# Decode step with attention and SwiGLU: layernorm steps on ScalarE, weight loads requeued, gate products moved, normalised input padded to 64 columns

## The chip, the cores and the metric

The kernel runs on one core of a Trainium2 chip. A core has TensorE (PE, matrix products; its weight loads are shown apart as PEld), VectorE (DVE), ScalarE (ACT), GpSimd (POOL) and SyncE (SP, which here issues DMAs and waits). Products land in PSUM, everything else lives in SBUF, and inputs come from HBM through 16 DMA engines. The metric is the device time of one execution in microseconds, as the median of several runs. One further execution is profiled; its span runs from the first instruction to the last.

## The reference

Four batch rows of one token each. The token is layer-normalised, and the result feeds an attention step over the last 4096 cached positions and a SwiGLU feed-forward; both are added to the input.

```python
B, D, F = 4, 512, 1792
Hq, Hkv, Sk, Dh = 32, 8, 16384, 128        # W = 4096, 4 query heads per K/V head
xn = (x - mean(x)) / sqrt(var(x) + 1e-5)
q  = (xn @ wq)                              # [B, Hq, Dh]
k, v = k_cache[:, :, Sk-W:, :], v_cache[:, :, Sk-W:, :]
o  = softmax(q k^T * Dh**-0.5) v
out = x + (o @ wo) + (silu(xn @ w_gate) * (xn @ w_up)) @ w_down
```

All inputs are bf16. K and V of the window are 33.5 MB each, W_q and W_o 4.2 MB each, and W_gate, W_up and W_down 1.8 MB each: some 81 MB, each byte read once.

## The kernel before

The order of work on every engine is written out by hand, and the engines meet through semaphores.

**Start.** ScalarE's queue loads x. VectorE sums x (L253), forms D*x - sum as `xc` (L255), ScalarE squares `xc` and accumulates (L239), VectorE forms the variance (L257), ScalarE takes the root (L241), VectorE the reciprocal (L259) and the scaled `xn` (L261). TensorE transposes `xn` in four pieces into PSUM (L336), VectorE copies them as `XnT` (L263), and TensorE multiplies 128 blocks of W_q with `XnT`, four columns each, into `q_ps` (L344). VectorE spreads q into `QZ` (L267), a table of 64-column blocks that are zero outside the 8 columns in use. Meanwhile GpSimd builds constants: masks, identity matrices, a zeroed `QZ` (L197); it raises `s_const` to 1 (L199), fills `P` with ones (L200), zeroes 12288 columns of `VB` (L201) and raises `s_const` to 2.

**The loop.** There are 32 pairs of batch row and K/V head, taken two at a time: `ND` = 16 steps, each with one 2 MB load of K and one of V. `KB` and `VB` hold two steps each. In one step TensorE transposes the first half of K (32 blocks, L357) while VectorE copies the results to `KT` (L276); takes the row maxima of the step before (L373); makes the second half of the products with V for two steps back, called PV here (L391, 64 moving columns each); makes the scores of the first half (L367); adds the shift by the maximum (L377), after which ScalarE takes the exponential (L244); and repeats transposes, PV and scores for the other halves. The first PV works on the ones and zeros that GpSimd left, and its end is the first count of `s_pv`. VectorE sums and inverts the denominators and scales the output into `OT` (`norm`, L290).

**The queue.** Nearly all loads go through SP's queue in one written order (L217 to L230): W_q, K of steps 0 and 1, W_down, V of step 0, then K and V in turn, the last V, W_gate, W_up and W_o in four pieces. Before each K from step 2 on, SP waits until both halves of the K two steps back are transposed (`s_tr`); before each V until the PV that frees its buffer has ended (`s_pv`). Everything further down the queue waits behind that.

**The end.** After the loop TensorE does the last maxima, the second half of PV for step 14, the shift for step 15, then all of PV for step 15 (L427, L428), the gate products (`up_gate`, L429: 56 blocks, four columns each, a weight block read with a stride of 14 elements), waits for the last normalisation (L430), transposes `OT` (L432) and regroups it (L438), makes the up products (L441), adds x, then multiplies W_down (L448) and W_o (L454), the latter as its four pieces land. VectorE copies the result out (L326), and two DMAs store it.

Of the kernel before, what the change touches and what calls it, by code (L numbers as in the profile page):

```python
# [3 lines left out]
BF16 = mybir.dt.bfloat16  # L4
FP32 = mybir.dt.float32
ALU = mybir.AluOpType
# [4 lines left out]
def bass_parallel_sum__sliding_block_cached__swiglu_ffn__decode_kernel(  # L11
# [18 lines left out]
    NC = D // 128  # L30
# [42 lines left out]
    xc = sb("xc", [B, D], FP32)  # L73
    xsq = sb("xsq", [B, D], FP32)
    xn = sb("xn", [B, D], FP32)
    st_sum = sb("st_sum", [B, 1], FP32)
    st_var = sb("st_var", [B, 1], FP32)
    st_std = sb("st_std", [B, 1], FP32)
    st_rstd = sb("st_rstd", [B, 1], FP32)
    XnT = sb("xnT", [128, NC, B], BF16)  # L80
    den = sb("den", [128, C], FP32)
    OT = sb("oT", [128, B, REP + HQ], BF16)
    OB = sb("oB", [32, B, Dh], BF16)
# [16 lines left out]
    O_wide = ps_O[:, 0:WIDE]  # L100
    den_ps = ps_O[:, 128:256]
    q_ps = ps_acc[:, 0:HQ * B]
    xT_ps = ps_acc[:, 128:128 + NC * B]
    mt_ps = ps_acc[0:C, 0:128]
    gate_ps = ps_kt[0][:, 0:NF * B]
    up_ps = ps_kt[1][:, 0:NF * B]
# [3 lines left out]
    def sem(name):  # L110
        return nc.alloc_semaphore(name=name)
# [12 lines left out]
    s_ss = sem("s_ss")  # L124
    s_var = sem("s_var")
    s_std = sem("s_std")
    s_xn = sem("s_xn")
    s_xT = sem("s_xT")
    s_xnT = sem("s_xnT")
# [36 lines left out]
    with nc.Block() as block:  # L166

        @block.gpsimd
        def _(eng):
            eng.memset(ident[:], 0.0)  # L170
            eng.memset(I4[:], 0.0)
            eng.memset(I8[:], 0.0)
            eng.memset(I4w[:], 0.0)
            eng.memset(rep[:], 0.0)
            eng.memset(ones[:], 1.0)
            eng.memset(mkr[:], -BIG)
            eng.memset(mkc[:], 1.0)
            eng.drain()
            eng.affine_select(I4[:], I4[:], pattern=[[-1, B]], compare_op=ALU.not_equal,
                              fill=1.0, base=0, channel_multiplier=1)  # L180
            eng.affine_select(ident[:], ident[:], pattern=[[-1, 128]], compare_op=ALU.not_equal,
                              fill=1.0, base=0, channel_multiplier=1)
            eng.affine_select(I8[:], I8[:], pattern=[[-1, C]], compare_op=ALU.not_equal,
                              fill=1.0, base=0, channel_multiplier=1)
            eng.affine_select(I4w[:], I4w[:], pattern=[[-1, 64]], compare_op=ALU.not_equal,
                              fill=1.0, base=0, channel_multiplier=1)

            eng.affine_select(rep[:], rep[:], pattern=[[1, REP], [-1, 128]], compare_op=ALU.not_equal,
                              fill=1.0, base=0, channel_multiplier=REP)

            eng.affine_select(mkr[:], mkr[:].rearrange("j (q b) -> j q b", b=2),
                              pattern=[[0, 64], [-1, 2]], compare_op=ALU.not_equal,
                              fill=0.0, base=0, channel_multiplier=1)
            eng.affine_select(mkc[:], mkc[:].rearrange("j (b h) -> j b h", b=2),
                              pattern=[[-1, 2], [0, REP]], compare_op=ALU.is_equal,
                              fill=0.0, base=0, channel_multiplier=1)
            eng.memset(QZ[:], 0.0)  # L197
            eng.drain()
            eng.engine_nop().then_inc(s_const, 1)  # L199
            eng.memset(P[:], 1.0)  # L200
            eng.memset(VB[:, HKN:], 0.0)  # L201
            eng.drain()
            eng.engine_nop().then_inc(s_const, 1)  # L203
            eng.engine_nop().then_inc(d_v[1], 16)

        @block.sync
        def _(eng):
            def load_k(d):
                if d >= 2:
                    eng.wait_ge(s_tr, 2 * NG * (d - 1))  # L210
                eng.dma_start(KB[:, d % 2 * KVN:(d % 2 + 1) * KVN], kv_ap(A_k_cache, d)).then_inc(d_k[d % 2], 16)

            def load_v(d):
                eng.wait_ge(s_pv, d + 1)
                eng.dma_start(VB[:, d % 2 * KVN:(d % 2 + 1) * KVN], kv_ap(A_v_cache, d)).then_inc(d_v[d % 2], 16)

            eng.dma_start(WQ[:], wq_ap).then_inc(d_wq, 16)  # L217
            load_k(0)
            load_k(1)
            eng.dma_start(WD[:], wd_ap).then_inc(d_wd, 16)  # L220
            load_v(0)
            for d in range(2, ND):
                load_k(d)
                load_v(d - 1)
            load_v(ND - 1)
            eng.dma_start(WG[:], wg_ap).then_inc(d_wg, 16)
            eng.dma_start(WU[:], wu_ap).then_inc(d_wu, 16)
            for n in range(len(d_wo)):
                a, b = WO_CUTS[n], WO_CUTS[n + 1]
                eng.dma_start(WO[:, a:b, :], wo_ap[:, a:b, :]).then_inc(d_wo[n], 16)  # L230
            eng.wait_ge(s_y, 1)
            eng.dma_start(out_ap[0], y[0:B, :]).then_inc(d_out, 16)
            eng.wait_ge(d_out, 32)

        @block.scalar
        def _(eng):
            eng.dma_start(X[:], x_ap).then_inc(d_x, 16)
            eng.wait_ge(s_xc, 1)
            eng.activation(xsq[:], xc[:], ACT.Square, accum_out=st_sum[:, 0:1]).then_inc(s_ss, 1)  # L239
            eng.wait_ge(s_var, 1)  # L240
            eng.activation(st_std[:], st_var[:], ACT.Sqrt).then_inc(s_std, 1)  # L241
            for d in range(-1, ND):
                eng.wait_ge(s_sh, d + 2)
                eng.activation(P[:, d % 2 * PS:d % 2 * PS + SN], ps_S[d % 2][:], ACT.Exp, scale=SCALE).then_inc(s_p, 1)  # L244
            eng.wait_ge(s_gate, 1)
            eng.activation(ex[:], gate_ps.rearrange("p (t b) -> p t b", b=B), ACT.Exp, scale=-1.0).then_inc(s_ex, 1)
            eng.wait_ge(s_y, 1)
            eng.dma_start(out_ap[1], y[64:64 + B, :]).then_inc(d_out, 16)

        @block.vector  # L250
        def _(eng):
            eng.wait_ge(d_x, 16)
            eng.tensor_reduce(st_sum[:], X[:], AX.X, ALU.add)  # L253
            eng.drain()
            eng.tensor_scalar(xc[:], X[:], float(D), st_sum[:, 0:1], ALU.mult, ALU.subtract).then_inc(s_xc, 1)  # L255
            eng.wait_ge(s_ss, 1)
            eng.tensor_scalar(st_var[:], st_sum[:], 1.0 / D, EPS * D * D, ALU.mult, ALU.add).then_inc(s_var, 1)  # L257
            eng.wait_ge(s_std, 1)
            eng.reciprocal(st_rstd[:], st_std[:])  # L259
            eng.drain()  # L260
            eng.tensor_scalar(xn[:], xc[:], st_rstd[:, 0:1], None, ALU.mult).then_inc(s_xn, 1)  # L261
            eng.wait_ge(s_xT, 1)
            eng.tensor_copy(XnT[:], xT_ps.rearrange("p (c b) -> p c b", b=B)).then_inc(s_xnT, 1)  # L263
            eng.wait_ge(s_const, 1)
            eng.wait_ge(s_q, 1)
            for bp in range(2):
                last = eng.tensor_copy(  # L267
# [61 lines left out]
        def _(eng):  # L329
            def mm(o, l, r, start=False, stop=True):  # L330
                return eng.matmul(o, l, r, start=start, stop=stop, skip_group_check=True)  # L331
# [9 lines left out]
            for c in range(NC):  # L341
                for h in range(HQ):
                    a = (c * HQ + h) * Dh
                    last = mm(q_ps[:, h * B:(h + 1) * B], WQ[:, a:a + Dh], XnT[:, c, :],  # L344
                              start=(c == 0 and h == 0))
            last.then_inc(s_q, 1)

# [32 lines left out]
            def pv(bank, s, n):  # L380
                p = bank * PS
                if s == 0:
                    eng.wait_ge(d_v[bank], n[0])
                    eng.wait_ge(s_p, n[1])
                    eng.wait_ge(s_nrm, n[1])
                    for j in range(SN // 128):
                        mm(den_ps, ones[:], P[:, p + 128 * j:p + 128 * (j + 1)], start=(j == 0))
                for t in range(HT):
                    a = bank * KVN + s * HKN + 128 * t
                    o = p + C * (s * HT + t)  # L390
                    last = mm(O_wide, VB[:, a:a + 128], P[:, o:o + WIDE], start=(s == 0 and t == 0))  # L391
                if s == 1:
                    last.then_inc(s_pv, 1)
# [24 lines left out]
            def up_gate(w, o, s, d):  # L418
                eng.wait_ge(d, 16)
                for t in range(NF):  # L420
                    for c in range(NC):
                        last = mm(o[:, t * B:(t + 1) * B],
                                  w[:].rearrange("p c (m t) -> p c t m", t=NF)[:, c, t, :], XnT[:, c, :],
                                  start=(t == 0 and c == 0))
                last.then_inc(s, 1)

            pv(1, 0, (8 * ND + 16, ND + 1))  # L427
            pv(1, 1, None)  # L428
            up_gate(WG, gate_ps, s_gate, d_wg)  # L429
            eng.wait_ge(s_nrm, ND + 2)  # L430
            for i in range(B):
                last = eng.transpose(  # L432
# [5 lines left out]
                last = mm(op_ps.rearrange("p (b c) -> p b c", b=B), rep[:, e, :], OB[:, :, 32 * e:32 * e + 32],  # L438
                          start=(e == 0))
            last.then_inc(s_pm, 1)  # L440
            up_gate(WU, up_ps, s_up, d_wu)  # L441
            for n in range(2):
                mm(ps_acc[64 * n:64 * n + 64, 0:256], I4w[:], X[:, 256 * n:256 * n + 256], start=True)
            eng.wait_ge(s_guT, 1)
# [39 lines left out]
```

## Time and profile before

| | |
|---|---|
| median of 3 runs | 205.23 us (204.55 to 206.20) |
| the profiled execution | 206.33 us |
| its span | 204.4 us |
| mean granted TensorE clock | 0.967 |
| PE busy | 171.0 us, 84% |
| PEld busy | 151.5 us, 74% |
| DVE busy | 124.9 us, 61% |
| ACT busy | 15.1 us, 7% |
| POOL busy | 16.6 us, 8% |
| read from HBM | 81.01 MB, 396 GB/s over the span |

In the profile, PE, PEld, DVE, ACT and POOL name the engines, and SPq and ACTq the places where a DMA is issued. A row of the timeline is: start and duration in us, engine, line of the kernel, operation, output <- inputs, count, and in brackets the idle time before it and what ended it. Consecutive instructions of one kind are merged into one row. The granted clock is the share of TensorE's full speed that it was allowed in a stretch. Durations of matmuls overlap, since they are pipelined.

### The profile page before, as it was taken

How to read it: one execution, taken by the hardware profiler on the slowest of the kernel's cores; microseconds unless marked ns; L12 is line 12 of the kernel's file. 1: busy time of each engine (PE TensorE's matmuls, PEld its weight loads, DVE VectorE, ACT ScalarE, POOL GpSimd, SP SyncE). 2: the span in 40 equal slices, each digit the busy share in tenths (PEclk: the TensorE clock that was granted, in tenths of full speed). 3: DMA queues.
4: the chain of work that ended last, by engine and by line, in shares of the span. 5: the costliest groups of instructions: out<-in, count | busy, mean ns of one | idle time of the engine just before them, and what ended most of it. 6: DMA issues, size and time to landing. Idle time of an engine off the chain costs nothing.

```text
span 204.4 us, 8087 instructions
## 1 busy us (share of the span) xinstructions
PE 171.0 (84%) x3634; PEld 151.5 (74%) x3634; DVE 124.9 (61%) x248; ACT 15.1 (7%) x24; POOL 16.6 (8%) x22
## 2 busy tenths in 40 slices
PE   0004899999998989889898989898989898979995
PEld 0004789898887978778887888787878787969853
DVE  4695366777776675857666767676767667531300
ACT  3500001101010101010010101010101010110000
POOL 8994000000000000000000000000000000000000
PEclk9999999999999999999999999999999999988559
DMA  7989928999999999999999999999999997899980
GB/s 257 449 385 439 419 85 366 427 406 443 414 443 430 417 446 420 446 427 420 446 417 449 423 427 439 417 449 423 433 436 417 446 423 337 314 422 435 423 358 8
DMA packets 5791, 81.12 MB, mean 397 GB/s; under 512 B 652, under 2 KB 664, under 8 KB 920
## 3 DMA queue, kind: packets, MB, share of 16 engines
q1 hardware_dynamic: 5768, 81.01, 93.6%
q8 instruction: 6, 0.10, 0.2%
q10 hardware_dynamic: 16, 0.01, 0.0%
q14 instruction: 1, 0.01, 0.0%
HBM read 81.01 MB, written 0.00 MB: 396 GB/s over the span
## 4 chain that ended last, share of the span: by engine, by line
DMA 43%; PE 43%; DVE 9%; issue 2%; ACT 1%; DVEq 0%
DMA kbuf<-in_A_k_cache_dram 43%; PE ps_kt L357 16%; PE ps_s L331 9%; PE ps_o L331 7%; PE ps_acc L331 6%; DVE xn L261 5%; PE ps_kt L331 4%; DVE kT L276 1%; DVE xc L255 1%; DMA x_sb<-in_A_x_dram 1%; ACT L241 1%; ACT xsq L239 0%; DVE rm L281 0%; DVE st_sum L253 0%; PE ps_acc L336 0%
## 5 line engine op out<-in xcount | busy, mean ns | idle before, releaser
L276 DVE COPY kT<-ps_kt 128x1024 bf16<-128x1024 bf16 x128 | 79.8, 684 | 24.5 <-PE ps_kt L357 24.5
L357 PE MATMUL ps_kt<-ident,kbuf 128*128 128x128 bf16 x1024 | 64.3, 222 | 8.8 <-DMA kbuf<-in_A_k_cache_dram 8.8
L357 PEld LDWEIGHTS ps_kt<-ident,kbuf 128*128 128x128 bf16 x1024 | 58.8, 99 | 14.1 <-issue 14.0
L331 PE MATMUL ps_o<-p,vbuf 128*128 128x64 bf16 x1120 | 40.4, 197 | 0.0
L331 PEld LDWEIGHTS ps_o<-p,vbuf 128*128 128x128 bf16 x1120 | 37.2, 101 | 1.2
L331 PEld LDWEIGHTS ps_s<-qz,kT 128*128 128x128 bf16 x1024 | 31.4, 98 | 6.9 <-issue 3.6
L331 PE MATMUL ps_s<-qz,kT 128*128 x1024 | 34.7, 192 | 1.3
L281 DVE TENSOR_REDUCE rm<-ps_s 128x8 bf16<-128x512 f32 x17 | 11.8, 692 | 19.6 <-PE ps_s L331 19.6
L244 ACT ACTIVATE p<-ps_s 128x512 bf16<-128x512 f32 x17 | 10.2, 597 | 163.7 <-PE ps_s L331 163.7
L336 PE MATMUL ps_acc<-i,xn 4*128 4x4 f32 x4 | 0.6, 254 | 18.0 <-DVE xn L261 18.0
L336 PEld LDWEIGHTS ps_acc<-i,xn 4*128 4x128 f32 x4 | 0.6, 207 | 18.0 <-POOLq L203 18.0
L261 DVE TENSOR_SCALAR xn<-xc,st_rstd 4x512 f32<-4x512 f32 x1 | 10.8, 10841 | 0.1
L201 POOL MEMSET vbuf<- 128x12288 bf16 x1 | 10.3, 10348 | 0.0
L331 PE MATMUL ps_o<-p,ones 128*128 128x128 bf16 (+1 forms) x69 | 7.0, 222 | 1.3 <-ACT p L244 0.7
L292 DVE TENSOR_REDUCE den<-ps_o 128x8 f32<-128x128 f32 x18 | 5.0, 275 | 5.0 <-PE ps_o L331 5.0
L331 PE MATMUL ps_s<-mkc,mkr 2*128 2x512 bf16 x17 | 6.8, 398 | 0.0
L331 PE MATMUL ps_s<-dg,ones 8*128 8x512 bf16 x17 | 6.5, 385 | 0.0
L331 PEld LDWEIGHTS ps_o<-p,ones 128*128 128x128 bf16 x69 | 4.6, 98 | 1.7 <-issue 1.7
L326 DVE CAST y_sb<-ps_acc 128x256 bf16<-128x256 f32 x1 | 0.4, 424 | 7.5 <-PE ps_acc L331 7.5
L286 DVE TENSOR_REDUCE m<-ps_acc 8x1 f32<-8x128 f32 x17 | 4.6, 270 | 0.3 <-PE ps_acc L331 0.3
L296 DVE TENSOR_TENSOR oT<-ps_o,den 128x8 f32 (+1 forms) x18 | 3.0, 167 | 2.9 <-issue 2.7
L331 PE MATMUL ps_acc<-wo_sb,oP 128*4 128x256 bf16 x64 | 4.5, 309 | 0.0
(61 smaller groups left out, 64.1 us busy)
## 6 DMA issues: line engine op xcount, KB each, us to landing
kbuf<-in_A_k_cache_dram SPq DMA_DIRECT2D x16, 2048.0 KB, 12.6
vbuf<-in_A_v_cache_dram SPq DMA_DIRECT2D x16, 2048.0 KB, 11.3
wq_sb<-in_A_wq_dram SPq DMA_DIRECT2D x1, 4096.0 KB, 12.2
wo_sb<-in_A_wo_dram SPq DMA_DIRECT2D x1, 2048.0 KB, 20.8
wd_sb<-in_B_w_down_dram SPq DMA_DIRECT2D x1, 1792.0 KB, 25.6
wg_sb<-in_B_w_gate_dram SPq DMA_DIRECT2D x1, 1792.0 KB, 11.6
wu_sb<-in_B_w_up_dram SPq DMA_DIRECT2D x1, 1792.0 KB, 16.4
wo_sb<-in_A_wo_dram SPq DMA_DIRECT2D x1, 1280.0 KB, 23.1
```

Source lines behind the costliest of these rows:

```text
L201: eng.memset(VB[:, HKN:], 0.0)
L241: eng.activation(st_std[:], st_var[:], ACT.Sqrt).then_inc(s_std, 1)
L244: eng.activation(P[:, d % 2 * PS:d % 2 * PS + SN], ps_S[d % 2][:], ACT.Exp, scale=SCALE).then_inc(s_p, 1)
L255: eng.tensor_scalar(xc[:], X[:], float(D), st_sum[:, 0:1], ALU.mult, ALU.subtract).then_inc(s_xc, 1)
L261: eng.tensor_scalar(xn[:], xc[:], st_rstd[:, 0:1], None, ALU.mult).then_inc(s_xn, 1)
L276: eng.tensor_copy(KT[:, u * HKN + 1024 * g:u * HKN + 1024 * (g + 1)], kt_ps[g].rearrange("p a b -> p (a b)")).then_inc(s_ev, 1)
L281: eng.tensor_reduce(RM[:], ps_S[bank][:].rearrange("p (t c) -> p c t", c=C), AX.X, ALU.max).then_inc(s_rm, 1)
L286: eng.tensor_reduce(m8[:], mt_ps, AX.X, ALU.max)
L292: eng.tensor_reduce(den[:], den_ps.rearrange("p (t c) -> p c t", c=C), AX.X, ALU.add)
L296: eng.tensor_tensor(OT[:, 2 * b:2 * b + 2, ds(r * REP, REP)], O_ps.rearrange("p (j h) -> p j h", j=2), den[:].rearrange("p (j h) -> p j h" ...
L331: return eng.matmul(o, l, r, start=start, stop=stop, skip_group_check=True)
L357: last = eng.transpose(kt_ps[g][:, k, :], KB[:, a:a + 128], ident[:])
```

## The change

- VectorE's sum is written negated (`st_neg`). ScalarE now forms `xc` (Identity, bias `st_neg`, scale D) and, after the reciprocal, `xn` (Identity, scale `st_rstd`). The semaphore `s_rs` hands the reciprocal over.
- `XnT` grows from 4 to 64 columns for each of four blocks; GpSimd zeroes it, VectorE fills the first four columns, now after waiting for `s_const`. The query, gate and up products take all 64 columns, and write 64 columns of which the last 60 add zeros into the neighbours' places. The transposes of `xn` land further up in their PSUM bank.
- GpSimd's clearing of `QZ` and `VB` is written as 4-byte elements, half as many.
- On SP's queue W_up takes W_down's place ahead of the first V, W_gate goes ahead of the last V, and W_down behind it.
- The gate products stand ahead of PV of step 15.

```diff
-    XnT = sb("xnT", [128, NC, B], BF16)
+    XnT = sb("xnT", [128, NC, WIDE], BF16)
...
-    xT_ps = ps_acc[:, 128:128 + NC * B]
+    xT_ps = ps_acc[:, 256:256 + NC * B]
...
-            eng.memset(QZ[:], 0.0)
+            eng.memset(XnT[:].bitcast(FP32), 0.0)
+            eng.memset(QZ[:].bitcast(FP32), 0.0)
...
-            eng.memset(VB[:, HKN:], 0.0)
+            eng.memset(VB[:, HKN:].bitcast(FP32), 0.0)
...
-            eng.dma_start(WD[:], wd_ap).then_inc(d_wd, 16)
+            eng.dma_start(WU[:], wu_ap).then_inc(d_wu, 16)
             load_v(0)
             for d in range(2, ND):
                 load_k(d)
                 load_v(d - 1)
+            eng.dma_start(WG[:], wg_ap).then_inc(d_wg, 16)
             load_v(ND - 1)
-            eng.dma_start(WG[:], wg_ap).then_inc(d_wg, 16)
-            eng.dma_start(WU[:], wu_ap).then_inc(d_wu, 16)
+            eng.dma_start(WD[:], wd_ap).then_inc(d_wd, 16)
...
             eng.wait_ge(s_xc, 1)
+            eng.activation(xc[:], X[:], ACT.Identity, bias=st_neg[:, 0:1], scale=float(D))
+            eng.drain()
             eng.activation(xsq[:], xc[:], ACT.Square, accum_out=st_sum[:, 0:1]).then_inc(s_ss, 1)
             eng.wait_ge(s_var, 1)
             eng.activation(st_std[:], st_var[:], ACT.Sqrt).then_inc(s_std, 1)
+            eng.wait_ge(s_rs, 1)
+            eng.activation(xn[:], xc[:], ACT.Identity, scale=st_rstd[:, 0:1]).then_inc(s_xn, 1)
...
-            eng.tensor_reduce(st_sum[:], X[:], AX.X, ALU.add)
-            eng.drain()
-            eng.tensor_scalar(xc[:], X[:], float(D), st_sum[:, 0:1], ALU.mult, ALU.subtract).then_inc(s_xc, 1)
+            eng.tensor_reduce(st_neg[:], X[:], AX.X, ALU.add, negate=True).then_inc(s_xc, 1)
...
-            eng.reciprocal(st_rstd[:], st_std[:])
-            eng.drain()
-            eng.tensor_scalar(xn[:], xc[:], st_rstd[:, 0:1], None, ALU.mult).then_inc(s_xn, 1)
+            eng.reciprocal(st_rstd[:], st_std[:]).then_inc(s_rs, 1)
             eng.wait_ge(s_xT, 1)
-            eng.tensor_copy(XnT[:], xT_ps.rearrange("p (c b) -> p c b", b=B)).then_inc(s_xnT, 1)
             eng.wait_ge(s_const, 1)
+            eng.tensor_copy(XnT[:, :, 0:B], xT_ps.rearrange("p (c b) -> p c b", b=B)).then_inc(s_xnT, 1)
...
-                    last = mm(q_ps[:, h * B:(h + 1) * B], WQ[:, a:a + Dh], XnT[:, c, :],
+                    last = mm(ps_acc[:, h * B:h * B + WIDE], WQ[:, a:a + Dh], XnT[:, c, :],
...
-                        last = mm(o[:, t * B:(t + 1) * B],
+                        last = mm(o[:, t * B:t * B + WIDE],
...
+            up_gate(WG, ps_kt[0], s_gate, d_wg)
             pv(1, 0, (8 * ND + 16, ND + 1))
             pv(1, 1, None)
-            up_gate(WG, gate_ps, s_gate, d_wg)
...
-            up_gate(WU, up_ps, s_up, d_wu)
+            up_gate(WU, ps_kt[1], s_up, d_wu)
```

More of the change, by code (lines that the diff above doesn't have):

```diff
@@ L75, in bass_parallel_sum__sliding_block_cached__swiglu_ffn__decode_kernel @@
     xn = sb("xn", [B, D], FP32)
+    st_neg = sb("st_neg", [B, 1], FP32)
     st_sum = sb("st_sum", [B, 1], FP32)
@@ L126, in bass_parallel_sum__sliding_block_cached__swiglu_ffn__decode_kernel @@
     s_std = sem("s_std")
+    s_rs = sem("s_rs")
     s_xn = sem("s_xn")
```

## The prediction

> **What bounds the kernel now.** The kernel reads 81 MB, so I begin with stretches of the span: PE, DVE, ACT and POOL busy time (count of instructions), granted TensorE clock, DMA share, GB/s.
>
> ```profile
> 2.00:26.00 24.00, 7.13 (x154) 6.35 (x155) 15.36 (x11) 4.18 (x6) 15.21 (x10) 1.00 0.97 412
> 26.00:33.00 7.00, 7.00 (x125) 6.13 (x124) 4.53 (x11) 0.60 (x1) 0.00 (x0) 1.00 0.38 127
> 33.00:172.00 139.00, 128.92 (x2884) 115.58 (x2881) 95.71 (x202) 8.36 (x14) 0.00 (x0) 1.00 1.01 431
> 172.00:178.00 6.00, 5.92 (x140) 5.24 (x140) 4.51 (x11) 0.60 (x1) 0.00 (x0) 1.00 0.67 249
> ```
>
> From 33 to 172 us the DMA engines are full (share 1.01, 431 GB/s), so nothing done to an engine there helps. There are two holes. The first loses 7 x (1 - 127/431) = 4.9 us of transfer, the second 6 x (1 - 249/431) = 2.5 us. Next, the timeline of the start says why the first hole exists (start, duration):
>
> ```profile
> 3.01 1.46 DVE L255 TENSOR_SCALAR xc<-x_sb,st_sum 4x512 f32<-4x512 bf16 x1
> ...
> 6.77 0.15 DVE L259 RECIPROCAL st_rstd<-st_std 4x1 f32<-4x1 f32 x1 [1.37 <-ACT st_std L241]
> 7.00 10.84 DVE L261 TENSOR_SCALAR xn<-xc,st_rstd 4x512 f32<-4x512 f32 x1
> 7.22 10.35 POOL L201 MEMSET vbuf<- 128x12288 bf16 x1
> ...
> 18.87 3.57 PE L331 MATMUL ps_acc<-xnT,wq_sb 128*128 128x4 bf16 x128 [0.27 <-DVE xnT L263]
> ...
> 23.89 3.59 PE L357 MATMUL ps_kt<-ident,kbuf 128*128 128x128 bf16 x32
> ...
> 27.62 1.55 PE L331 MATMUL ps_o<-p,vbuf 128*128 128x64 bf16 x32
> ...
> 29.20 0.54 SPq L215 DMA_DIRECT2D vbuf<-in_A_v_cache_dram  x1
> ```
>
> A 4x512 scaling takes 10.84 us and ends with GpSimd's 10.35 us memset. The query products follow, then the first 32 key transposes, then the dummy PV, whose end lets SP issue the first V at 29.20. By then the queue is dry. Next, the issues (KB, us from issue to landing), and the issue times of W_q and of W_o's pieces (first and last):
>
> ```profile
> wq_sb<-in_A_wq_dram SPq DMA_DIRECT2D x1, 4096.0 KB, 12.2
> ...
> wo_sb<-in_A_wo_dram SPq DMA_DIRECT2D x1, 256.0 KB, 23.9
> ```
> ```profile
> 0.80 0.41 SPq L217 DMA_DIRECT2D wq_sb<-in_A_wq_dram  x1
> ```
> ```profile
> L230 SPq DMA_DIRECT2D wo_sb<-in_A_wo_dram x4: 441/458/686, 174.8 to 176.5; - x4
> ```
>
> W_q lands at 0.80 + 12.2 = 13.0, six microseconds before the query products begin. Last, the chain of waits at the end (start, length) and the timeline of the tail:
>
> ```profile
> 157.21 12.59 DMA kbuf<-in_A_k_cache_dram
> ...
> 181.33 0.61 ACT p L244
> ...
> 182.02 3.80 PE ps_o L331 x68
> 185.82 3.33 PE ps_kt L331 x56
> ...
> 194.64 7.47 PE ps_acc L331 x80
> ```
> ```profile
> 169.92 1.96 PE L357 MATMUL ps_kt<-ident,kbuf 128*128 128x128 bf16 x32 [0.76 <-DMA kbuf<-in_A_k_cache_dram]
> ...
> 171.96 1.11 PE L331 MATMUL ps_o<-p,vbuf 128*128 128x64 bf16 x32
> ...
> 180.91 0.39 PE L331 MATMUL ps_s<-dg,ones 8*128 8x512 bf16 x1
> ...
> 189.08 0.60 PE L432 MATMUL ps_kt<-ident,oT 128*32 128x128 bf16 x4
> ...
> 190.74 3.52 PE L331 MATMUL ps_kt<-xnT,wu_sb 128*128 128x4 bf16 x56
> ```
>
> The last K lands at 169.80; from there TensorE's own chain runs to 202.1 with short waits, so the end is set by when the last K lands plus that chain. The last piece of W_o lands at 176.5 + 23.9 = 200.4, 1.7 us before the chain's end: close behind, but not the bound.
>
> **Layernorm on ScalarE.** It removes the 1.46 and the 10.84 from VectorE. In their place stand two ScalarE passes over 4x512. The nearest row is the square of the same shape:
>
> ```profile
> 4.50 0.63 ACT L239 ACTIVATE xsq<-xc 4x512 f32<-4x512 f32 x1 [1.81 <-DVE xc L255]
> 5.04 0.19 ACT L239 ACTIVATION_READ_ACCUMULATOR xsq<-xc 4x1 f32 x1
> 5.24 1.28 ACT L241 ACT_TABLE_LOAD   x1
> ```
>
> The sum of x is ready just before 3.01. Then 0.63 (centre), 0.63 + 0.19 (square), 1.28 (table), 0.25 for the root (from the table's end at 6.52 to 6.77), 0.15 (reciprocal) and 0.63 (scale) reach 6.8. Transposes and copy add 1.0 (from xn's end at 17.84 to 18.87), and xnT stands near 8. The third table load now follows the scale on ScalarE, and nothing needs it until the first exp. A second pass as dear as 1.46 would still leave 3 us before W_q lands: cost nothing, cover W_q's transfer.
>
> ```profile
> 6.23 1.06 POOL L200 MEMSET p<- 128x1152 bf16 x1
> ```
>
> VectorE now waits for the constants ahead of the xnT copy. Queued behind it are only the copies of q. GpSimd adds one small memset (xnT) and writes QZ in 4-byte elements; its constants were done before this memset of p began, so the wait is over by 8. The large memset lies between half of 10.35 and all of it, ends between 12 and 17.6, and is needed only by the dummy PV past 20. Cost nothing.
>
> The rule that speaks here: the Trainium skill, SBUF — State Buffer, "Who interferes with whom", says that VectorE and GpSimd share a port pair as an exclusive lock, taken by a scaling with source and result in SBUF, and not by an operation with one SBUF input or less outside the two-port modes. The 10.84 beside 10.35 agrees; for the xnT copy, which reads PSUM, no row shows it, since before it ran at a time when GpSimd was idle.
>
> **xn padded to 64 columns.** Two rows of the tail, and the same tail in stretches; the granted clock is the figure after PE busy:
>
> ```profile
> 182.25 3.58 PE L331 MATMUL ps_o<-p,vbuf 128*128 128x64 bf16 x64
> 185.66 3.49 PE L331 MATMUL ps_kt<-xnT,wg_sb 128*128 128x4 bf16 x56
> ```
> ```profile
> 178.82:182.24 3.42, 1.90 (x44) 1.00 0.98 421
> 182.24:185.65 3.41, 3.41 (x68) 0.50 1.01 433
> 185.65:189.06 3.41, 3.41 (x61) 1.00 1.02 429
> 189.06:192.48 3.42, 2.91 (x39) 0.50 1.01 435
> ...
> 199.30:202.10 2.80, 2.78 (x50) 1.00 0.03 12
> ```
>
> 128 query products cost 28 ns each with 4 columns (3.57/128). With 64 columns the nearest rows are PV: 1.11/32 = 35 ns at full clock; at half clock (182.24 to 185.65) 3.58/64 = 56 ns. So 4.4 to 7.2 us in place of 3.57. The clock column reads 1.00 that early, but 32 transposes take 3.59 at 23.89 and 1.96 at 169.92, so I take TensorE for cold at 13.0; the dense padded products should wake it part-way: I take 6.2.
>
> **The first hole.** Query products start at 13.05 and end at 19.3 (17.5 to 20.3). Before, V was issued 29.20 - 22.44 = 6.8 us after their end, on a TensorE still cold (transposes 3.59). At full clock the same steps take 1.96 and 1.11 in place of 3.59 and 1.55, so 4.7. The first V is issued near 24.0 (22.2 to 27.1). With a loss of 4.9 us for an issue at 29.20, no transfer is lost for an issue up to 24.3, and each later microsecond costs one. So the hole closes: -4.9 us (bound -2.1), and since the queue is full from there to the last K, the last K lands 4.9 us earlier, at 164.9. W_up in W_down's place is of the same 1792 KB, so V, waiting behind it on SP, sees no change.
>
> **W_gate ahead of the last V.** The second hole is SP waiting for a buffer for the last V with nothing else queued; 1792 KB at 431 GB/s is 4.3 us and covers 2.5; its issue falls into time in which SP would wait anyway. The last W_o lands near 200.4 - 7.4 = 193.0. That alone is worth nothing as long as TensorE ends later. W_down, behind the last V now, lands some 4.3 us after it, about 184, and its products come past 188.
>
> **Gate products ahead of the last PV.** The normalisation's last row:
>
> ```profile
> 186.50 0.17 DVE L296 TENSOR_TENSOR oT<-ps_o,den 128x8 bf16<-128x8 f32 x1
> ```
>
> Before: shift ends 181.30, then exp (0.61), PV 3.80, gate 3.33 (hiding the normalisation), then transposes. After: shift ends near 176.4, gate 3.5 to 179.9 hiding exp and the last V. That V comes 2 x 2048 + 1792 KB behind the last K, 14.0 us by 431 GB/s, so 178.9. Then PV, then the normalisation bare: its 0.85 us behind PV's end (185.82 to 186.67), and some 0.1 until the next products start. 0.95 is added and exp with its hand-over (181.30 to 182.02) goes: +0.25.
>
> **The tail's clock.** The clock falls after a stretch of sparse work (178.82) and again after the gate stretch, which is busy throughout but with 4-column products of 62 ns (3.49/56). So columns count, not busy time. At 64 columns each product streams about 30 ns of its 62 (from 1.96/32 = 61 ns for 128 columns), which is neither the dense loop nor the 4-column case. Products of 62 ns stay 62 at both clocks (3.49 full, 3.52 half), so they are bound by the weight load and the padding costs 0 there. At full clock PV costs 2 x 1.11 + 0.3 = 2.5 in place of 3.8, and the W_down and W_o products 92 x 2.80/50 = 5.2 in place of 7.47: at most -3.6 together, at least 0. I take -2.0, somewhat over half, since the padded products should win back some stretches.
>
> **Sum.** -4.9 + 0.25 - 2.0 = -6.7. The profiled execution (span 204.4 in 206.33 us) becomes 199.7; the median 205.23 becomes 198.5. Floor: TensorE cannot end before the last W_o at 193.0 plus its last four products (0.2), so -8.9: 196.3.
>
> **Rivals.**
> A. *Hole closed, tail clock partly mended*: 196.3 to 200.4, likeliest 198.5. Chance 0.69.
> B. *Hole closed, clock as before*: half-filled products don't count as dense. -4.65: 200.6, and up to 203.4 if the first V is as late as 27.1. For it: the fall after 178.82 came with 1.90 of 3.42 us busy. Chance 0.16.
> C. *The wait moves instead of going*: the xnT copy stands behind the large memset, which isn't shortened. It ends by 17.57; the copy's 0.17 and cold query products of 6.2 to 7.2 end at 24 to 25, and 4.7 later the first V goes out at 28.7 to 29.7: the hole stays. +0.25 and the clock's 0 to -3.6 are left: 201.9 to 205.5. Against it: the reciprocal at 6.77 ran in 0.15 beside GpSimd's memset of p, in the row shown. Chance 0.08. By the port rule named above it would not happen.
> D. *Slower*: the padded column stream doesn't hide behind the strided weight load of gate and up. Then 62 ns becomes up to 62 + 56 = 118: 112 x 56 ns = 6.3 us on the path, against -4.65: +1.6, 206.9. It decides from 42 ns a product, and with the hole only partly closed (-2.1) it reaches 209.7. Against it: query products of 28 ns at 4 columns and PV of 35 at 64 differ by 7 ns, less than the 30 of the stream, so streams and loads do overlap. Chance 0.07. The Trainium skill, TensorE: Matmul & The Clock Gate, Part 3 ("What overlaps and what doesn't"), has weight loads overlap only where row groups differ; by it every product here would be serial, and the 35 ns disagrees.
>
> **Numbers.** Predicted 198.5. The range takes A and B but for B's late V: 196.3 to 201.8. About 1% (2 us) is what a measurement here tells from no change. Faster by over 1%: A, B but for its slow edge, and the fast edges of C and D, 0.89; within: 0.07, the rest of C and D's milder prices; slower: 0.04, from D.
>
> **What would show it.** Right: xn a ScalarE row under 1 us; query products starting at W_q's landing near 13; first V issued by 24.5; 26 to 33 us above 400 GB/s; no dip near 170; last K near 165; TensorE's last product near 195 with less half clock. Wrong: query products past 16 (C), gate rows well over 62 ns (D), a half clock through W_down (B), or a last K that isn't earlier although the hole closed, which would mean that the loop and not the queue sets its pace.

## The result, and the profile after

| | before | after |
|---|---|---|
| median | 205.7 us (4 runs) | 198.82 us (4 runs, 197.16 to 199.52) |
| profiled execution, span | 206.33, 204.4 us | 199.46, 197.6 us |
| last K lands | 169.80 us | 165.15 us |
| last product ends | 202.1 us | 195.3 us |

The ratio to the kernel before is 0.966, 95% interval 0.958 to 0.974. Predicted were 198.5 us and a range of 196.3 to 201.8. Where the profiled execution of a kernel lay well above its others (e5: 202.28 us beside 199.8 to 200.7; e8: 201.49 beside 198.3 to 199.2), its tail is not read.

The changed kernel's stretches (engine busy times, granted clock, DMA share, GB/s) show both holes gone: 396 GB/s in place of 127 and 437 in place of 249.

```profile
26.00:33.00 7.00, 6.92 (x169) 6.34 (x166) 5.77 (x12) 0.00 (x0) 0.00 (x0) 1.00 1.01 396
...
172.00:178.00 6.00, 5.13 (x125) 4.58 (x123) 3.02 (x8) 0.60 (x1) 0.00 (x0) 1.00 1.02 437
```

The timeline of its start, in order of time (start, duration), says how the first hole closed:

```profile
6.14 5.22 POOL L204 MEMSET vbuf<- 128x6144 f32 x1
...
6.71 0.72 ACT L248 ACTIVATE xn<-xc,st_rstd 4x512 f32<-4x512 f32 x1 [0.22 <-DVE st_rstd L264]
...
8.23 0.17 DVE L267 CAST xnT<-ps_acc 128x16 bf16<-128x16 f32 x1 [1.55 <-PE ps_acc L339]
...
13.16 6.02 PE L334 MATMUL ps_acc<-xnT,wq_sb 128*128 128x64 bf16 x128 [4.97 <-DMA wq_sb<-in_A_wq_dram]
...
20.24 1.96 PE L360 MATMUL ps_kt<-ident,kbuf 128*128 128x128 bf16 x32
...
23.42 0.54 SPq L218 DMA_DIRECT2D vbuf<-in_A_v_cache_dram  x1
```

xn takes 0.72 us beside the memset, where it took 10.84. The bracket behind the query products now names W_q's transfer. The copy of xnT runs in its usual 0.17 in the middle of the memset, so the wait has not moved there. The transposes run at full clock, 1.96 for 32, and the first V goes out 5.8 us earlier.

The tail, as the chain of waits and as TensorE's timeline:

```profile
152.57 12.58 DMA kbuf<-in_A_k_cache_dram
...
180.19 2.10 PE ps_o L334 x68
...
188.39 6.94 PE ps_acc L334 x92
```
```profile
176.58 3.61 PE L334 MATMUL ps_kt<-xnT,wg_sb 128*128 128x64 bf16 x56
180.02 0.39 PE L334 MATMUL ps_o<-p,ones 128*128 128x128 bf16 x4
180.25 2.03 PE L334 MATMUL ps_o<-p,vbuf 128*128 128x64 bf16 x64
183.18 0.40 PE L435 MATMUL ps_kt<-ident,oT 128*32 128x128 bf16 x4 [0.90 <-DVE oT L299]
184.08 0.39 PE L334 MATMUL ps_kt<-oB,rep 32*128 32x128 bf16 x4 [0.51 <-DVE oB L316]
184.40 3.61 PE L334 MATMUL ps_kt<-xnT,wu_sb 128*128 128x64 bf16 x56
```

PV of the last step is down from 3.80 to 2.10 and the W_down and W_o products from 7.47 to 6.94. A padded gate product costs 64 ns (3.61/56) where the narrow one cost 62. The normalisation now stands bare, 0.90 ahead of the transposes. The granted clock (the figure after TensorE's busy time) still falls once:

```profile
178.32:181.74 3.42, 3.42 (x87) 1.00 1.01 425
181.74:185.15 3.41, 2.00 (x39) 1.00 1.01 435
185.15:188.56 3.41, 3.38 (x53) 0.50 0.97 411
188.56:191.98 3.42, 3.42 (x36) 0.50 0.84 341
191.98:195.35 3.37, 3.33 (x60) 1.00 0.05 21
```

The fall follows the stretch with the two waits, in which TensorE was busy 2.00 of 3.41 us.

### The profile page after: what moved, and what is told of

Read it like the earlier page. It is cut to its first block, busy times and chain, and to the rows that moved or that the text cites. A ratio compares the mean times of both kernels' runs of the same rounds, so it can differ in the third digit from the quotient of the medians.

```text
span 197.6 us, 8087 instructions
## 1 busy us (share of the span) xinstructions
PE 168.7 (85%) x3634; PEld 150.1 (76%) x3634; DVE 112.0 (57%) x246; ACT 16.6 (8%) x26; POOL 10.4 (5%) x23
## 4 chain that ended last, share of the span: by engine, by line
DMA 51%; PE 43%; DVE 3%; issue 2%; DVEq 0%
DMA kbuf<-in_A_k_cache_dram 45%; PE ps_kt L360 16%; PE ps_s L334 9%; PE ps_acc L334 8%; PE ps_o L334 6%; DMA wq_sb<-in_A_wq_dram 6%; PE ps_kt L334 4%; DVE kT L279 1%; DVE rm L284 0%; DVE y_sb L329 0%; DVE oB L316 0%; PE ps_kt L435 0%; DVE den L295 0%; DVE qz L270 0%; DVE den L297 0%
## 5 line engine op out<-in xcount | busy, mean ns | idle before, releaser
L360 PE MATMUL ps_kt<-ident,kbuf 128*128 128x128 bf16 x1024 | 62.7, 220 | 10.0 <-DMA kbuf<-in_A_k_cache_dram 10.0
L360 PEld LDWEIGHTS ps_kt<-ident,kbuf 128*128 128x128 bf16 x1024 | 57.2, 98 | 15.0 <-issue 15.0
L334 PE MATMUL ps_o<-p,vbuf 128*128 128x64 bf16 x1120 | 38.4, 194 | 0.0
L334 PEld LDWEIGHTS ps_o<-p,vbuf 128*128 128x128 bf16 x1120 | 35.2, 98 | 1.1
L334 PE MATMUL ps_acc<-xnT,wq_sb 128*128 128x64 bf16 x128 | 6.0, 227 | 5.0 <-DMA wq_sb<-in_A_wq_dram 5.0
L334 PEld LDWEIGHTS ps_acc<-xnT,wq_sb 128*128 128x128 bf16 x128 | 5.9, 122 | 5.0 <-issue 5.0
L204 POOL MEMSET vbuf<- 128x6144 f32 x1 | 5.2, 5222 | 0.0
## 6 DMA issues: line engine op xcount, KB each, us to landing
wd_sb<-in_B_w_down_dram SPq DMA_DIRECT2D x1, 1792.0 KB, 14.4
```

The source lines that it names most:

```text
L204: eng.memset(VB[:, HKN:].bitcast(FP32), 0.0)
L360: last = eng.transpose(kt_ps[g][:, k, :], KB[:, a:a + 128], ident[:])
```

## The experiments

Each kernel was timed beside the kernel before on the same chip; ratios to it stand with their 95% intervals.

### The start: which part closes the first hole

**e1: only layernorm moved.** The kernel before with the diff's ScalarE and VectorE lines of the layernorm and nothing else.

> The kernel before with one thing changed: the two layernorm passes run on ScalarE. GpSimd's long memset stays as it was, 12288 two-byte elements. Theory (the first hole in the transfers comes from the scaling that waits for GpSimd's memset): xn ends near 7.5, the query products start when W_q lands, near 13.1, and with 4 columns take 3.6; the first K lands near 17.9; the first V is issued near 23.5, the stretch from 26 to 33 us moves at least 390 GB/s, the last K lands near 165 and the time falls by about 4.9 us, to about 200.8. Rival 1 (the pads and the new queue carry the gain): no change, 205.7. Rival 2 (the wait moves to the xnT copy, which then stands beside the long memset until 17): query products start past 17, gain under 1.5 us.

Measured: 201.09 us, ratio 0.978 (0.973 to 0.983). Its timeline, and its stretches:

```profile
13.15 3.55 PE L333 MATMUL ps_acc<-xnT,wq_sb 128*128 128x4 bf16 x128 [5.16 <-DMA wq_sb<-in_A_wq_dram]
...
23.66 0.54 SPq L217 DMA_DIRECT2D vbuf<-in_A_v_cache_dram  x1
```
```profile
26.00:33.00 7.00, 6.92 (x165) 6.34 (x163) 5.77 (x11) 0.00 (x0) 0.00 (x0) 1.00 1.00 413
...
165.00:171.00 6.00, 6.00 (x122) 5.27 (x123) 4.04 (x10) 0.60 (x1) 0.00 (x0) 1.00 0.68 251
```

The first hole is gone, the second (165 to 171 here) is still there, and the gain is 4.7 us. The xnT copy again took 0.17, here beside the long memset. Both rivals fall. In the tail the up products wait for W_up, and the chain that ended last runs through that transfer:

```profile
186.06 3.52 PE L333 MATMUL ps_kt<-xnT,wu_sb 128*128 128x4 bf16 x56 [0.26 <-DMA wu_sb<-in_B_w_up_dram]
```

**e2: only the memset shortened.**

```diff
-            eng.memset(VB[:, HKN:], 0.0)
+            eng.memset(VB[:, HKN:].bitcast(FP32), 0.0)
```

> The kernel before with one thing changed: GpSimd clears VB as 6144 four-byte elements in place of 12288 two-byte ones (5.2 us in the changed kernel, 10.35 before). Layernorm stays on VectorE. Theory: the scaling still waits for the memset, but only until about 12.5, query products start near 14, end near 17.6, the first V is issued near 24 and the gain is the same as that of the whole start, about 4.9 us, to about 200.8, so that moving layernorm is not needed for it. Rival (layernorm on VectorE is slow by itself): xn still takes about 10 us and the time stays at 205.7.

Measured: 201.52 us, ratio 0.981 (0.976 to 0.986). The scaling on VectorE:

```profile
7.00 5.72 DVE L261 TENSOR_SCALAR xn<-xc,st_rstd 4x512 f32<-4x512 f32 x1
```

It follows the memset down from 10.84 to 5.72 us, which shows that the memset and not the scaling made it long. The query products start at 13.75, the first V goes out at 23.71, and the gain of 4.3 us is that of e1 within the intervals. Either edit closes the hole by itself: the last K lands at 164.9 us in e1, at 165.5 in e2 and at 165.15 in the changed kernel, which has both.

**e3: the changed kernel with the old start.** The layernorm lines of e1 and the memset of e2 undone.

> The changed kernel with its start undone: layernorm on VectorE and VB cleared as two-byte elements; padding, queue and gate order as changed. Theory: xn ends near 17, query products run from 18 to 24, the first V is issued near 28.5 to 29.5 and the first hole is back with 4 to 5 us lost; the second hole stays closed. Time 203 to 204.5, which is 4 to 5 us over the changed kernel's 198.8. Rival (closing the second hole and the earlier weights carry the gain): within 1.5 us of the changed kernel.

Measured: 202.87 us, ratio 0.986 (0.981 to 0.991), 4.0 us over the changed kernel. From its timeline, and its stretches:

```profile
6.72 10.55 DVE L264 TENSOR_SCALAR xn<-xc,st_rstd 4x512 f32<-4x512 f32 x1
...
28.70 0.54 SPq L218 DMA_DIRECT2D vbuf<-in_A_v_cache_dram  x1
```
```profile
26.00:33.00 7.00, 7.00 (x155) 6.27 (x153) 5.74 (x14) 0.60 (x1) 0.00 (x0) 1.00 0.45 158
```

Wait, late V and hole are back together, and the rest of the change keeps 2.9 us against the kernel before.

### The tail: padding, queue and order

**e4: no padding.** The three `mm` calls take `XnT[:, c, 0:B]` and write `B` columns; the rest is the changed kernel.

> The changed kernel with 4 columns again in the query, gate and up products; all else as changed. Theory: after the gate products the granted clock falls, PV of the last step takes 3.6 to 3.8 in place of 2.1, and the W_down and W_o products stay at half clock for longer; time 1 to 3 us over the changed kernel's 198.8, so 199.8 to 201.8. The start loses nothing, since the query products end earlier but the first K lands only near 17.9. Rival (padding is worth nothing, because the clock falls in the tail either way): within 0.5 us of 198.8.

Measured: 201.38 us, ratio 0.977 (0.971 to 0.983), 2.6 us over the changed kernel and no better than e1. Its tail:

```profile
176.00 3.52 PE L334 MATMUL ps_kt<-xnT,wg_sb 128*128 128x4 bf16 x56
179.38 0.59 PE L334 MATMUL ps_o<-p,ones 128*128 128x128 bf16 x4
179.76 3.62 PE L334 MATMUL ps_o<-p,vbuf 128*128 128x64 bf16 x64
```

```profile
174.00:177.40 3.40, 2.91 (x57) 0.99 1.01 434
177.40:180.80 3.40, 3.40 (x60) 0.50 0.97 411
180.80:184.20 3.40, 2.58 (x49) 0.50 1.02 437
```

PV is back at half-clock cost. In the stretches (TensorE's busy time, granted clock, DMA share, GB/s) the clock falls at 177.4, after 1.4 us of narrow gate products, although TensorE was busy for 2.91 of 3.40 us, and the trace has half clock from there to 194.4.

**e5: the old queue and the old place of the gate products,** with start and padding as changed.

```diff
-            eng.dma_start(WU[:], wu_ap).then_inc(d_wu, 16)
+            eng.dma_start(WD[:], wd_ap).then_inc(d_wd, 16)
             load_v(0)
...
-            eng.dma_start(WG[:], wg_ap).then_inc(d_wg, 16)
             load_v(ND - 1)
-            eng.dma_start(WD[:], wd_ap).then_inc(d_wd, 16)
+            eng.dma_start(WG[:], wg_ap).then_inc(d_wg, 16)
+            eng.dma_start(WU[:], wu_ap).then_inc(d_wu, 16)
...
-            up_gate(WG, ps_kt[0], s_gate, d_wg)
             pv(1, 0, (8 * ND + 16, ND + 1))
             pv(1, 1, None)
+            up_gate(WG, ps_kt[0], s_gate, d_wg)
```

> The changed kernel with the queue's order and the gate's place of the kernel before (W_down ahead of the first V, W_gate and W_up behind the last; gate products behind the last PV). Layernorm on ScalarE, short memset and padding stay. Theory: the last K lands as in the changed kernel, near 165; the second hole of 2.5 us is back but lies beside TensorE's chain; W_up lands near 186 and the up products wait for it by up to 1.5 us, or the last W_o, near 195.5 to 196, sets the end. Time 0.5 to 2.5 us over the changed kernel's. Rival (the queue's order is worth nothing, since TensorE's chain sets the end): the same within 0.5 us. Rival (closing the second hole brings its 2.5 us in full): 2.5 us or more.

Measured: 200.25 us, ratio 0.974 (0.968 to 0.981), 1.4 us over the changed kernel and inside the range of the theory. In its profiled execution the transfers were thin early on (262 GB/s from 36 to 38 us), and the last K landed at 167.2, so e11 is the same kernel once more, beside e10, the changed kernel once more.

> The kernel of the earlier run with the old queue and the old place of the gate products, since the profiled execution of that one lost 2 us of transfers near 35 us that its other executions may not have lost. Theory (the second hole lies beside TensorE's chain, and its cost is W_gate's and W_up's lateness at the tail): the last K lands near 165, the gate products wait for W_gate by about 1 us and the up products for W_up by 0.2 to 0.5 us, and the time is 1.0 to 2.0 us over the changed kernel's. Rival (queue and gate order are worth nothing): within 0.5 us.

Measured: 200.51 us, ratio 0.975 (0.970 to 0.979), 2.5 us over e10's 197.98 and above the range of the theory. The chain of waits of e11, one of its stretches, and two rows of its TensorE timeline:

```profile
170.46 23.01 DMA wo_sb<-in_A_wo_dram
...
193.52 1.81 PE ps_acc L334 x28
```
```profile
165.00:171.00 6.00, 6.00 (x125) 5.27 (x123) 4.20 (x11) 0.60 (x1) 0.00 (x0) 1.00 0.86 303
```
```profile
180.05 3.64 PE L334 MATMUL ps_kt<-xnT,wg_sb 128*128 128x64 bf16 x56 [0.85 <-DMA wg_sb<-in_B_w_gate_dram]
...
193.52 2.21 PE L334 MATMUL ps_acc<-wo_sb,oP 128*4 128x256 bf16 x32 [0.55 <-DMA wo_sb<-in_A_wo_dram]
```

The lateness of W_gate (0.85 us) and of W_up (0.24) was as expected, but what sets the end is something else: TensorE waits for pieces of W_o, and the chain is a transfer up to 193.5. The last piece lands at 171.5 + 23.8 = 195.3, which is 2.2 us behind e10's 193.1 (below), and its products end at 195.7. The second hole, 303 GB/s from 165 to 171, loses 6 x (1 - 303/431) = 1.8 us in this trace and has moved the end of all transfers; the span is 198.0 us beside e10's 196.1. The queue's moves were not run one by one, nor the old queue with the gate products ahead of PV.

**e6: gate products late, queue as changed.** Only the last of the three parts of e5's diff.

> The changed kernel with the gate products behind the last PV, as before; the queue as changed. Theory: PV then waits for the last V, which lands near 179 to 180, instead of running gate products meanwhile; PV ends near 182, the gate products of 3.6 hide the normalisation's 0.9, so the transposes start near 185.7 in place of 183.2: 1.5 to 2.5 us over the changed kernel's. Rival (by the sum of the prediction the place of the gate products is worth only 0.25 us, with the last V on time in either order): within 0.5 us.

Measured: 200.83 us, ratio 0.979 (0.972 to 0.986), 2.0 us over the changed kernel. In its timeline PV waits for the last V:

```profile
178.68 0.61 PE L334 MATMUL ps_o<-p,ones 128*128 128x128 bf16 x4 [2.54 <-DMA vbuf<-in_A_v_cache_dram]
```

Behind W_gate the last V lands at 178.6. The gate products of the changed kernel fill just this wait; without them TensorE stands still and the clock falls before PV (3.62 again).

**e7: 128 columns in the gate and up products.** `XnT` is 128 wide, and `up_gate` writes 128 columns.

> The changed kernel with gate and up products padded to 128 columns (the query products stay at 64). Theory (the clock follows the share of time in which columns stream): at full clock a product streams 61 of its 62 to 64 ns, the stretches of gate and up count as dense, the half clock from 185 to 192 us goes, W_down and W_o take about 5.2 in place of 6.9 and the time falls by 0 to 1.7 us. Rival 1 (the clock falls for the gaps around the normalisation and the regrouping, whatever the columns): the same half-clock stretch at the tail, and with 128 columns at half clock each product costs about 110 ns, so up to 2.5 us slower. Rival 2 (streams do not hide behind the weight load): 3 us slower or more even at full clock.

Measured: 198.35 us, ratio 0.964 (0.956 to 0.971): no difference from the changed kernel that these runs resolve. From its timeline:

```profile
184.28 5.10 PE L334 MATMUL ps_kt<-xnT,wu_sb 128*128 128x128 bf16 x56
...
189.75 1.69 PE L334 MATMUL ps_acc<-wd_sb,guT 128*4 128x256 bf16 x28
```

The clock falls at 185.4, in the up products, as rival 1 has it; there the wide products cost up to 1.5 us more, but the clock is back at 188.8 instead of 192.0, and W_down takes 1.69 in place of 3.15. The two cancel in this trace. That the width won the clock back isn't shown: in e10 it was back at 189.0 with 64 columns. The gate products, at full clock, took 3.66 with 128 columns: streams hide behind the weight load, and rival 2 falls.

**e8: another filler ahead of the first V.** `WO_CUTS` is (0, 10, 20, 30, 32); the first piece of W_o goes where W_up was, and W_up behind the last V.

> The changed kernel with another filler ahead of the first V: 1280 KB of W_o in place of W_up's 1792 KB; W_up goes behind the last V, ahead of W_down, and the rest of W_o follows in pieces of 1280, 1280 and 256 KB. Theory (the end is the last K's landing plus TensorE's chain, and all that is queued ahead of the last K delays it): the last K lands 0.8 to 1.2 us earlier, W_up lands just before its products need it, and the time falls by 0.5 to 1.2 us until the last W_o at 193.5 binds. Rival (the smaller filler leaves a hole before the first V, or W_up and W_down come late): no gain, or slower by up to 2 us.

Measured: 198.56 us, ratio 0.967 (0.961 to 0.974), no gain over the changed kernel. Its one trace, read ahead of the tail, speaks for the first half of the rival: it moved 392 GB/s from 20 to 26 us and 374 from 26 to 33, where the changed kernel moved 428 and 396. That loses 0.9 us, most of the 1.2 that 512 KB less take at 431 GB/s, and the last K lands at 164.7, no earlier than in other kernels with the full filler (164.6 in e4, 165.3 in e9). Whether W_up and W_down also come late is left open.

**e9: up products ahead of the normalisation's wait.** Behind PV the order is: up products, transposes, residual, half of W_down, regrouping, other half, W_o.

```diff
             pv(1, 1, None)
+            up_gate(WU, ps_kt[1], s_up, d_wu)
             eng.wait_ge(s_nrm, ND + 2)
...
+            down(range(0, 7))
             eng.wait_ge(s_ob, 1)
...
-            up_gate(WU, ps_kt[1], s_up, d_wu)
...
+            down(range(7, NF))
```

> The changed kernel with another order behind the last PV: up products first (W_up is there since the start), then the transposes of the output, the residual and half of W_down's products, the regrouping, the other half, then W_o; VectorE's steps follow that order. Theory (the end is TensorE's chain behind the last K, and its gaps for the normalisation, 0.9 us, and for the copy between transposes and regrouping, 0.5 us, are on it): both gaps are covered, W_o's products end 1.0 to 1.8 us earlier than the changed kernel's, until the last W_o's landing at 193.4 binds; time 197.0 to 198.0 beside 198.5 for the changed kernel. Rival (the transfers already set the end, since the last W_o lands at 193.4 and TensorE ends at 195.3): less than 0.5 us. A longer unbroken stretch of TensorE work should also leave less half clock.

**e10: the changed kernel once more.**

> The changed kernel as it is, as a measure for the others of this call: 198 to 199.5. The granted clock of its tail differs from run to run, with the spans between 195.5 and 198.

Measured: e9 198.55 us, ratio 0.966 (0.961 to 0.971); e10 197.98 us, ratio 0.962 (0.959 to 0.966). The theory falls and the rival holds, although everything in e9's tail went as wanted. The mean granted clock was 1.0 in five of e9's six executions and in two of e10's six. In e9's profiled execution it was full throughout; two stretches of it (TensorE's busy time, granted clock, DMA share, GB/s), and TensorE's timeline:

```profile
182.20:185.60 3.40, 3.40 (x64) 1.00 1.00 427
185.60:189.00 3.40, 2.79 (x42) 1.00 0.98 411
```
```profile
182.25 3.55 PE L334 MATMUL ps_kt<-xnT,wu_sb 128*128 128x64 bf16 x56
185.73 0.40 PE L436 MATMUL ps_kt<-ident,oT 128*32 128x128 bf16 x4
...
186.28 0.93 PE L334 MATMUL ps_acc<-wd_sb,guT 128*4 128x256 bf16 x14
...
187.46 0.93 PE L334 MATMUL ps_acc<-wd_sb,guT 128*4 128x256 bf16 x14
189.02 1.91 PE L334 MATMUL ps_acc<-wo_sb,oP 128*4 128x256 bf16 x32 [0.62 <-DMA wo_sb<-in_A_wo_dram]
191.97 2.20 PE L334 MATMUL ps_acc<-wo_sb,oP 128*4 128x256 bf16 x32 [1.04 <-DMA wo_sb<-in_A_wo_dram]
```

The gaps are covered, W_o's products start at 189.0 instead of 191.3 (190.1 in e10), and then wait for W_o twice. They end at 194.2. In e10, with half clock in one stretch only, they end at 193.8:

```profile
188.26 2.03 PE L334 MATMUL ps_acc<-wd_sb,guT 128*4 128x256 bf16 x28
190.13 3.66 PE L334 MATMUL ps_acc<-wo_sb,oP 128*4 128x256 bf16 x64
```
```profile
L233 SPq DMA_DIRECT2D wo_sb<-in_A_wo_dram x4: 432/432/432, 169.6 to 171.0; - x4
...
DMA to landing us min/median/max: 18.6/21.6/22.1
```

The last piece of W_o lands at 171.0 + 22.1 = 193.1 in e10. So the changed kernel already ends within 0.7 us of its transfers with one stretch at half clock, and within 1.9 with two (195.3 beside 171.1 + 22.3 = 193.4 in its first trace). No version here is measurably faster.

## Why the prediction was right, and where not

The forecast of -6.7 us met a measured -6.9 (205.7 to 198.8), and -7.7 in e10. By its steps:

- **First hole.** Right in mechanism and size. xnT stood at 8.4 (near 8 was said), the query products took 6.02 (6.2), the first V went out at 23.42 (24.0), the last K landed at 165.15 (164.9), 4.65 us earlier. e1, e2 and e3 tie it to the scaling's wait for GpSimd's memset. Moving the layernorm was priced as if it alone did this; e2 shows that the memset's form did it as well, so that 4.9 is the price of either and not of both. The wider query products took 2.5 us more than in e4 (6.02 beside 3.55), but the key transposes behind them ran in 1.96 instead of 3.59, and the first V went out no later (23.42 beside 23.76).
- **The wait on the xnT copy (rival C)** didn't come: 0.17 beside the memset in the changed kernel and in e1. The rule cited for it from the Trainium skill (SBUF — State Buffer, "Who interferes with whom"), by which such a copy isn't blocked, agrees with that.
- **Padding.** 0 was said for gate and up; they went from 62 to 64 ns, 0.2 us for both. Rival D needed 42 ns more a product. The rule of the Trainium skill (TensorE: Matmul & The Clock Gate, Part 3, "What overlaps and what doesn't") that would have made load and stream serial doesn't hold here: 128 columns cost 65 ns (e7) where 4 cost 62, both at full clock. Rival D's own argument was weaker: it set 28 ns of the start, where the transposes took 3.59, beside 35 ns at full clock.
- **The tail's clock.** -2.0 was said. In the profiled execution it was 3.80 - 2.10 = 1.7 at PV plus 7.47 - 6.94 = 0.5, so -2.2; in e10 it was 1.7 plus 1.9, where 1.9 is 7.47 less the chain's 5.54 (188.26 to 193.79). The -2.0 was a choice between -3.6 and 0, and two traces of one kernel lie at -2.2 and -3.6, so that it fits so well is partly luck. Without the padding (e4) 2.6 us come back. The reason, that columns count and not busy time, is supported by two stretches in which TensorE was busy throughout: behind the narrow gate products of the kernel before (185.65 to 189.06) the clock fell, behind the padded up products of e9 (182.20 to 185.60) it held. Waits count as well: in e11 it fell at 182.5, in padded gate products that had begun at 180.05 behind a wait of 0.85 us. So the stretch with the two waits is the likely cause of the half clock that is left in the changed kernel; e9, which fills both, had full clock in five executions of six. But the changed kernel had it too in some, so this is not shown.
- **Gate ahead of PV.** From the shift's end to the transposes' start the tail takes 183.18 - 176.65 = 6.5 us, before 7.8; less the 1.7 that the clock gave PV, that is some +0.45 where +0.25 was said. But the step set its new place against the old kernel only. In the new queue the old place costs 2.0 us (e6), since the last V now lands behind W_gate. Queue and order belong together.
- **W_gate ahead of the last V: the step that failed.** The prediction said that closing the second hole "is worth nothing as long as TensorE ends later". It took TensorE's end from the sum in which the clock is mended, 195, and the last W_o from the queue in which the hole is closed, 193.0, and never set the mended tail against the unmended queue: 193.0 + 2.5 = 195.5, later than TensorE. e11 is that case: the last W_o lands at 195.3 and sets the end, and 1.9 us of span are lost (2.5 between the medians of e11 and e10, 1.4 between those of e5 and the changed kernel). The total came out right because the change does both. (A slip without consequence in the same step: 178.9 + 4.3 is 183.2 and not "about 184"; W_down landed at 169.0 + 14.4 = 183.4.) A row of the kernel before shows how near the transfers already were, since the weight loads of its up products start only when W_up lands:

```profile
190.74 3.44 PEld L331 LDWEIGHTS ps_kt<-xnT,wu_sb 128*128 128x128 bf16 x56 [0.21 <-DMA wu_sb<-in_B_w_up_dram]
```

The last points explain why the parts don't add up. On top of the mended start (e1, 201.09), queue and gate order without padding give +0.3 (e4), padding without them -0.6 (e11), and both together -2.3 (the changed kernel; -3.1 by e10). These are differences of medians whose intervals are 0.7 to 1.7 us wide to either side, so the first two can't be told from nothing; the bound that took over is seen in the traces. At half clock TensorE ends after the transfers (in e4 at 197.2, where the last W_o lands near 193.0), and with the hole the transfers set the end (e11).

## What to carry to other kernels

When two chains end within a few per cent of each other, price an edit to one of them against the other chain as it will be after the change and as it is now, since either may be the floor. A hole in the transfers is worth its length only where no other chain ends later: here the first was worth 4.0 to 4.7 us, the second nothing measurable beside half-clock products (e4) and some 2 us beside the mended tail (e11). It is found by following SP's wait back to the engine that is late; for the first hole that was a 4x512 scaling standing behind a memset on another engine. Before moving work to another engine to get out of such a wait, try to shorten what it waits for.

## What the runs showed of the hardware

- GpSimd's memset goes by elements, not bytes: 12288 two-byte elements took 10.35 us, the same bytes as 6144 four-byte ones 5.22. VectorE's scaling beside it lasted 10.84 and 5.72; VectorE's reciprocal of 4x1 and its copy out of PSUM weren't held up (0.15 and 0.17).
- A product whose weights are read with a stride of 14 elements takes 62 to 65 ns at full clock whether 4, 64 or 128 columns stream (3.49, 3.61 and 3.66 us for 56), against 28 ns for 4 columns with contiguous weights (3.57 us for 128 at the start). The weight loads show the same (3.44 us for 56, 3.49 for 128). No run changed the stride alone.
- TensorE's clock fell in spite of a busy engine: in e4 it stayed at half speed for the 17 us to 194.4, in which TensorE was never idle for more than 0.9 us at a time, and in the kernel before it fell behind 3.41 us of narrow products without a gap. The share of streamed columns at which it falls or comes back wasn't measured.
